# Seven products of half matrices for eight in the down projection of a fused retention and gated feed-forward kernel

## The chip, the cores and the metric

The kernel runs on one core of a Trainium2 chip. The metric is device time in microseconds. TensorE (PE) multiplies matrices into PSUM, VectorE (DVE) and ScalarE (ACT) read PSUM and write SBUF, GpSimd (POOL) and SyncE (SP) here mostly issue transfers. Each engine takes its instructions strictly in the order in which the kernel wrote them (PE may load weights a little ahead), and waits at semaphores for the others.

## The reference

```
gamma = 1.0 - 2.0 ** (-5.0 - arange(H))                     # B, H, S, D = 4, 8, 768, 64
for t in range(S):
    state = gamma * state + outer(k[:, :, t], v[:, :, t])
    y[:, :, t] = scale * q[:, :, t] @ state
x = y.transpose(0, 2, 1, 3).reshape(3072, 512)
gate = 1.0 / (1.0 + exp(-(x @ w_gate)))                     # w_gate, w_val: 512 x 1536
out = (gate * (x @ w_val)) @ w_out                          # w_out: 1536 x 512
```

Inputs and output are float32; the kernel multiplies in bfloat16 and sums in float32.

## The kernel before

Retention is computed in 24 chunks of 128 tokens (four batches of six), the feed-forward part in six tiles of 512 tokens, four chunks to a tile. A tile has 12 up groups, `up(t, n1)`: eight products of 512 columns into two PSUM banks (gate and value), a sigmoid on ACT into `gs`, and a product on DVE into `hT[t][:, n1]`, the transposed hidden rows in bfloat16. Then come eight down groups: for each of four blocks of 128 tokens two halves of six products of 512 columns into one bank (L316), a copy on ACT into `ob` (L321) and a store on SP. The last block of the last tile is computed by `last_down` in pieces of 256, 128 and 128 columns (L336), copied by DVE, ACT and DVE.

The attention work for later tiles is put between these groups by the table `plan`: an entry `(i, block, done, new)` runs after group `i`. `block(done, new)` finishes two chunks (`inter` L190 and `intra` L237 on PE, then `y_out` L245 on DVE, which writes a quarter of the next tile's `xT` each) and begins two others (`scores` L178 and `state` L196 on PE, `masks` L183 and L184 and `state_sum` L222 to L226 on DVE). On DVE the order in a block with both is the two `y_out`, four masks, the state sums. `casts` (L202) has ACT write the summed state into `zbd`, which later `inter` products read. `step_t` transposes a chunk on PE, copies it on ACT into `qkT` (L151), and scales `v` on DVE into `vs` (L169); from chunk 12 on SP's transfers do the transposes (`xbar`) and POOL the scaling. Chunk loads are issued by POOL.

Seven PSUM banks serve everything but the states, in rotation: the eighth request waits until the readers of the first are through. `gs` has three buffers, `hT` two, `ob` three. The order of instructions is written out by hand; no scheduler changes it. In tile 0 the first four up groups run ahead of the loop, so that its groups 0 to 7 are up and 8 to 15 down; in tile 1 the first ten up groups are done in two halves of 256 columns, the second half by `up_columns` (L299), 25 groups in all.

Of the kernel before, what the change touches and what calls it, by code (L numbers as in the profile page):

```python
# [17 lines left out]
def kernel(  # L18
# [22 lines left out]
    ctx.enter_context(tc.manual_schedule())  # L41
    const = ctx.enter_context(tc.tile_pool(name="const", bufs=1))
    wpool = ctx.enter_context(tc.tile_pool(name="wpool", bufs=1))
    ld = ctx.enter_context(tc.tile_pool(name="ld", bufs=12))
    at = ctx.enter_context(tc.tile_pool(name="at", bufs=2))
    ffn = ctx.enter_context(tc.tile_pool(name="ffn", bufs=3))
    pz = ctx.enter_context(tc.tile_pool(name="pz", bufs=1, space=bass.MemoryType.PSUM))
# [4 lines left out]
    NT = N_TOK // 512  # L52
# [23 lines left out]
    wo = wpool.tile([128, NFF, D_MODEL], BF16, name="wo")  # L76
# [9 lines left out]
                            in_=moe_w_out.rearrange("(n p) d -> p n d", p=128)[:, s * 3:(s + 1) * 3, :])  # L86


    kf = const.tile([C, H, D], F32, name="kf")
    qf = const.tile([C, H, D], F32, name="qf")  # L90
    nc.sync.dma_start(out=kf, in_=src(k, 0))
    nc.sync.dma_start(out=qf, in_=src(q, 0))
    nc.scalar.preload_act_table(AX.Exp)
# [42 lines left out]
    xT, vs, qkT, sc, stA, stB, y, zbds = {}, {}, {}, {}, {}, {}, {}, {}  # L136
    zz, za = {}, {}

    def bank(shape, dt=F32):
        return pf.tile(shape, dt, tag="ff", name="ff", padded_shape=[128, 2 * NP, C] if dt == BF16 else None)  # L140
# [18 lines left out]
            nc.scalar.activation(qkT[g][:, i * NP:(i + 1) * NP], tp, AX.Copy)  # L159

    def xbar(g):
        qkT[g] = ld.tile([128, 2 * NP, C], BF16, tag="qkX", name="qkX", bufs=8)
        for i, x in enumerate((kn[g], qn[g])):
            nc.sync.dma_start_transpose(out=qkT[g][:, i * NP:(i + 1) * NP, :],
                                        in_=x.rearrange("s h d -> s (h d)"))

    def scale_v(g, eng):
        vs[g] = ld.tile([C, H, D], BF16, tag="vs", name="vs", bufs=8)
        eng.tensor_tensor(vs[g], vf[g], tabv[:, g % NCH, :].unsqueeze(2).to_broadcast([C, H, D]),  # L169
                          op=ALU.mult)  # L170

# [104 lines left out]
    hT = {}  # L276
# [15 lines left out]
    def up_columns(t, n1s, lo, hi):  # L292
        n = hi - lo
        ps = []
        for w in (wg, wv):
            u = bank([128, 512])
            for i, n1 in enumerate(n1s):
                for kk in range(KT):
# [6 lines left out]
        nc.vector.tensor_tensor(hT[t][:, n1s[0]:n1s[-1] + 1, lo:hi], g.rearrange("p (i n) -> p i n", n=n),  # L305
                                ps[1].rearrange("p (i n) -> p i n", n=n), op=ALU.mult)

    po = {}

    def down(t, sm, part):  # L310
        if part == 0:
            po[0] = bank([128, 512])
        o = po[0]
        half = NFF // 2
        for n1 in range(part * half, (part + 1) * half):
            nc.tensor.matmul(o, hT[t][:, n1, sm * 128:(sm + 1) * 128], wo[:, n1, :],  # L316
                             start=(n1 == 0), stop=(n1 == NFF - 1))
        if part == 0:
            return
        ob = ffn.tile([128, D_MODEL], F32, tag="ob", name="ob")  # L320
        nc.scalar.copy(ob, o)  # L321
        row = t * 512 + sm * 128
        nc.sync.dma_start(out=out[row:row + 128, :], in_=ob)

    def keep_on(n):
        u = bank([128, 512])
        for _ in range(n):
            nc.tensor.matmul(u[:, :128], ident, ident, start=True, stop=True)  # L328

    def last_down(t):  # L330
        row = t * 512 + 384
        first = 0
        for i, width in enumerate((256, 128, 128)):
            o = bank([128, 512])
            for n1 in range(NFF):
                nc.tensor.matmul(o[:, :width], hT[t][:, n1, 384:512], wo[:, n1, first:first + width],  # L336
                                 start=(n1 == 0), stop=(n1 == NFF - 1))
            ob = ffn.tile([128, width], F32, tag=f"ob{width}", name="ob", bufs=2)
            if i == 1:
                nc.scalar.copy(ob, o[:, :width])  # L340
                nc.scalar.dma_start(out=out[row:row + 128, first:first + width], in_=ob)
            else:
                nc.vector.tensor_copy(ob, o[:, :width])
                nc.sync.dma_start(out=out[row:row + 128, first:first + width], in_=ob)
            first += width


    scale_v(0, nc.gpsimd)
# [64 lines left out]
    def ups(t):  # L413
        return [lambda n1=n1: up(t, n1) for n1 in range(NFF)]

    def downs(t):
        return [lambda sm=sm, i=i: down(t, sm, i) for sm in range(4) for i in range(2)]

    plan = {
        0: [(9, step_t, 4), (11, step_t, 5), (12, block, None, 4), (12, casts, 4), (13, step_t, 6), (14, block, 4, None)],  # L420
        1: [(0, step_t, 7), (2, block, None, 6), (3, step_t, 8), (4, casts, 6), (5, step_t, 9), (7, block, 6, 8),
            (9, casts, 8), (11, step_t, 10), (13, step_t, 11), (15, block, 8, 10), (17, casts, 10), (20, block, 10, None)],
        2: [(1, block, None, 12), (3, casts, 12), (7, block, 12, 14), (9, casts, 14), (16, block, 14, 16), (18, casts, 16)],
        3: [(6, block, 16, 18), (8, casts, 18), (15, block, 18, 20), (17, casts, 20)],
        4: [(6, block, 20, 22), (8, casts, 22), (14, block, 22, None)],
        5: [],
    }
    for t in range(NT):
        groups = ups(t) + downs(t)
        if t == NT - 1:  # L430
            groups[-2:] = [lambda: last_down(t)]
        if t == 0:
            groups = groups[4:]
            for g in range(8, 12):
                load_chunk(g)
        if t == 1:
            groups[:10] = [lambda n1=n1: up(1, n1, 0, 256) for n1 in range(10)]
            groups[10:10] = [lambda n1=n1: up_columns(1, range(n1, n1 + 2), 256, 512) for n1 in range(0, 10, 2)]
            for g in range(12, 16):
                load_chunk(g)  # L440
        if t == 2:
            scale_v(14, nc.gpsimd)
            scale_v(15, nc.gpsimd)
            load_chunk(18)
            scale_v(16, nc.gpsimd)
            scale_v(17, nc.gpsimd)
            load_chunk(19)
        if t == 3:
            for g in range(18, 22):
                scale_v(g, nc.gpsimd)  # L450
            load_chunk(22)
# [50 lines left out]
```

## Time and profile before

| | |
|---|---|
| time, three runs | 234.22 us median, 233.8 to 235.6 |
| span of the profiled execution | 232.9 us (its own time on the device is the span and about a microsecond around it; the median is 1.3 above) |
| PE busy | 222.9 us, 96% of the span |
| DVE, ACT, POOL busy | 110.0, 91.8, 92.2 us |
| up products (L285), 512 columns | 452 recorded, 379 ns each with overlap |
| down products (L316), 512 columns | 267 recorded, 379 ns each with overlap |
| TensorE clock granted | full throughout |

In the views, a line such as `L316 PE MATMUL ff<-wo,hT` names the kernel's line, the engine, the operation, and what is written from what; `ff` is any of the seven banks. A matmul's length includes its way through the array, which overlaps the next one, so the distance between starts is its price. "Idle before" names what ended the engine's idle time. In the chain of waits, each row has a start, a length and the work; in the timeline, rows of one kind that follow each other are merged.

### The profile page before, as it was taken

Reading aid. Unit: us, or ns where it says so; the run is one execution under the profiler, and the core shown is the slowest. Engines: PE = TensorE matmul, PEld = TensorE weight load, DVE = VectorE, ACT = ScalarE, POOL = GpSimd, SP = SyncE. Lnnn points to the kernel's source line nnn. Section 1 sums busy time; section 2 is a strip of 40 time slices with the busy share of each in tenths; the row PEclk is TensorE's granted clock in tenths of the full one; section 3 lists DMA queues with packets and bytes.
Section 4 is the critical chain, followed back from the end, with each engine's and each line's share of the span. In section 5 each row is a group of like instructions: output and inputs, shape, how many; then the busy total and the mean of one; then the engine's idle time right before and its main releaser. Section 6 shows DMA issues by size and latency. Waiting matters only on the chain.

```text
span 232.9 us, 4448 instructions
## 1 busy us (share of the span) xinstructions
PE 222.9 (96%) x1781; PEld 125.5 (54%) x1802; DVE 110.0 (47%) x201; ACT 91.8 (39%) x177; POOL 92.2 (40%) x111
## 2 busy tenths in 40 slices
PE   6878999999999999999999999999999999999994
PEld 5654644557889645445445445445445454444444
DVE  4465533275996562284924445716236711244301
ACT  8765233354727332253522432522532422433221
POOL 8999864788899743495118200000000000000000
PEclk9999999999999999999999999999999999999999
DMA  7999999999999999999959953001200011100022
GB/s 135 187 188 173 197 202 204 183 234 231 215 175 155 114 114 125 276 180 143 107 70 160 205 101 61 1 30 63 91 0 3 0 45 69 69 0 0 0 93 90
DMA packets 77557, 27.29 MB, mean 117 GB/s; under 512 B 65057, under 2 KB 73121, under 8 KB 77537
## 3 DMA queue, kind: packets, MB, share of 16 engines
q0 software_dynamic: 57616, 16.78, 75.9%
q1 hardware_dynamic: 19776, 10.16, 22.2%
q8 instruction: 14, 0.23, 0.4%
q10 hardware_dynamic: 144, 0.07, 0.1%
q14 instruction: 7, 0.05, 0.1%
HBM read 28.31 MB, written 6.29 MB: 149 GB/s over the span
## 4 chain that ended last, share of the span: by engine, by line
PE 84%; POOL 6%; DMA 3%; issue 2%; DVE 2%; ACT 1%; POOLq 0%
PE ff L285 46%; PE ff L316 25%; PE ff L299 5%; DMA wv<-in_moe_w_val_dram 3%; PE ff L237 2%; PE ff L178 2%; PE ff L190 2%; PE ff L149 1%; PE ff L336 1%; POOL qn L68 1%; POOL kn L67 1%; PE z L196 1%; POOL vf L62 1%; POOL vs L169 1%; POOL wg L81 1%
## 5 line engine op out<-in xcount | busy, mean ns | idle before, releaser
L290 DVE TENSOR_TENSOR hT<-gs,ff 128x512 bf16<-128x512 f32 (+2 forms) x72 | 45.6, 641 | 69.4 <-PE ff L285 57.1
L285 PE MATMUL ff<-xT,wg 128*128 128x512 bf16 (+2 forms) x277 | 68.0, 361 | 1.4 <-DVE xT L245 0.7
L285 PE MATMUL ff<-xT,wv 128*128 128x512 bf16 (+2 forms) x287 | 68.6, 361 | 0.7 <-DMA wv<-in_moe_w_val_dram 0.6
L289 ACT ACTIVATE gs<-ff 128x512 f32<-128x512 f32 (+2 forms) x72 | 40.2, 562 | 68.0 <-PE ff L285 62.0
L316 PE MATMUL ff<-wo,hT 128*128 128x512 bf16 x267 | 61.1, 379 | 0.9 <-issue 0.5
L285 PEld LDWEIGHTS <-wv 128*128 128x128 bf16 x288 | 28.1, 98 | 29.8 <-DMA wv<-in_moe_w_val_dram 0.9
L316 PEld LDWEIGHTS <-hT 128*128 128x128 bf16 x276 | 26.3, 98 | 31.3 <-DVE hT L290 0.6
L285 PEld LDWEIGHTS <-wg 128*128 128x128 bf16 x288 | 27.1, 98 | 28.5 <-issue 0.7
L321 ACT COPY ob<-ff 128x512 f32<-128x512 f32 x23 | 13.5, 585 | 51.1 <-PE ff L316 38.2
L245 DVE TENSOR_TENSOR xT<-ff,taby 128x512 bf16<-128x512 f32 x24 | 15.6, 686 | 25.9 <-PE ff L237 25.9
L169 POOL TENSOR_TENSOR vs<-vf,tabv 128x512 bf16<-128x512 f32 x14 | 14.7, 1060 | 26.0 <-DMA vf<-in_v_dram 22.9
L62 POOL DMA_DIRECT2D vf<-in_v_dram x23 | 20.8, 904 | 8.1 <-DMA kn<-in_k_dram 2.8
L67 POOL DMA_DIRECT2D kn<-in_k_dram x23 | 21.0, 912 | 3.2 <-DMA wo<-in_moe_w_out_dram 1.1
L68 POOL DMA_DIRECT2D qn<-in_q_dram x23 | 20.5, 892 | 3.1 <-DMA wo<-in_moe_w_out_dram 2.2
L183 DVE TENSOR_TENSOR stA<-ff,causal 128x512 bf16<-128x512 f32 x24 | 16.3, 681 | 2.7 <-PE ff L178 2.6
L184 DVE TENSOR_TENSOR stB<-ff,causal 128x512 bf16<-128x512 f32 x24 | 16.3, 679 | 0.0
L202 ACT CAST zbd<-za 64x256 bf16<-64x256 f32 x32 | 12.9, 403 | 8.6 <-DVE za L224 8.0
L169 DVE TENSOR_TENSOR vs<-vf,tabv 128x512 bf16<-128x512 f32 x10 | 7.3, 734 | 5.0 <-DMA vf<-in_v_dram 4.9
L151 ACT ACTIVATE qkT<-ff 128x1024 bf16<-128x1024 bf16 x8 | 8.2, 1026 | 1.6 <-PE ff L149 1.6
L328 PE MATMUL ff<-ident 128*128 128x128 bf16 x82 | 7.3, 254 | 1.6 <-POOL ident masks.py:199 1.6
L237 PE MATMUL ff<-stB,vs 128*64 128x128 bf16 x96 | 7.9, 222 | 0.4 <-DVE stB L184 0.4
L237 PE MATMUL ff<-stA,vs 128*64 128x128 bf16 x96 | 8.1, 222 | 0.0
(62 smaller groups left out, 141.5 us busy)
## 6 DMA issues: line engine op xcount, KB each, us to landing
vf<-in_v_dram POOLq DMA_DIRECT2D x23, 256.0 KB, 8.0
out_dram<-ob SPq DMA_DIRECT2D x23, 256.0 KB, 3.1
kn<-in_k_dram POOLq DMA_DIRECT2D x23, 128.0 KB, 7.8
qn<-in_q_dram POOLq DMA_DIRECT2D x23, 128.0 KB, 8.0
wg<-in_moe_w_gate_dram POOLq DMA_DIRECT2D x6, 256.0 KB, 7.5
wv<-in_moe_w_val_dram POOLq DMA_DIRECT2D x6, 256.0 KB, 8.0
wo<-in_moe_w_out_dram POOLq DMA_DIRECT2D x4, 384.0 KB, 11.4
kf<-in_k_dram SPq DMA_DIRECT2D x1, 256.0 KB, 3.4
```

What stands on the lines that cost most here:

```text
L62: eng.dma_start(out=vf[g], in_=src(v, g))
L67: nc.gpsimd.dma_start(out=kn[g], in_=src(k, g))
L68: nc.gpsimd.dma_start(out=qn[g], in_=src(q, g))
L169: eng.tensor_tensor(vs[g], vf[g], tabv[:, g % NCH, :].unsqueeze(2).to_broadcast([C, H, D]), op=ALU.mult)
L183: nc.vector.tensor_tensor(stA[g], sc[g][0], causal4, op=ALU.mult)
L184: nc.vector.tensor_tensor(stB[g], sc[g][1], causal4, op=ALU.mult)
L237: nc.tensor.matmul(y[g][i * D:(i + 1) * D, p, :], vs[g][:, 2 * p + i, :], st[:, p, :], start=(first and p == 0), stop=True, skip_group_che ...
L245: nc.vector.tensor_tensor(xT[g // 4][:, :, col:col + C], y[g], taby[:, :, c * C:(c + 1) * C], op=ALU.mult)
L285: nc.tensor.matmul(u[:, lo:hi], w[:, kk, n1 * 128:(n1 + 1) * 128], xT[t][:, kk, lo:hi], start=(kk == 0), stop=(kk == KT - 1))
L289: nc.scalar.activation(gs[:, lo:hi], ps[0][:, lo:hi], AX.Sigmoid)
L290: nc.vector.tensor_tensor(hT[t][:, n1, lo:hi], gs[:, lo:hi], ps[1][:, lo:hi], op=ALU.mult)
L316: nc.tensor.matmul(o, hT[t][:, n1, sm * 128:(sm + 1) * 128], wo[:, n1, :], start=(n1 == 0), stop=(n1 == NFF - 1))
```

## The change

From tile 1 on the down projection is done on half matrices. The 512 token columns of `hT` are split in halves of 256, the 12 row blocks into even and odd ones, and the 512 output columns into halves. With a11, a21 the even blocks of the first and second token half, a12, a22 the odd ones, b11, b12 the even blocks of `w_out` for the first and second half of the columns, and b21, b22 the odd ones, seven products of 6 x 256 columns are made for each of two token sub-blocks i, and the four quarters of the output are sums of them. `weight_sums` prepares four combinations of `w_out` in tile 0 (three calls, each for four blocks, with four operations on DVE and two copies on ACT). `hidden_sums` prepares three combinations of the hidden rows in `hs` and overwrites a21 by a11 - a21 (three calls a tile, four DVE operations each). `product` adds several products into the same bank, and `fast_out` takes intermediate values out of it: after product 2 a copy `p` of the bank on ACT and a sum on DVE, after 6 a copy and a sum and the first store, after 7 a sum, after 4 a copy and the second store.

There are now seven down groups in tiles 1 to 5, two products each. `last_down` is gone. In `plan`, the blocks of tiles 1 to 4 stand after other groups. `ld` has 11 buffers for 12, `qkX` and `vs` have 7 for 8, `ob` has 4 for 3, two of them used first by `kf` and `qf`.

```diff
-    ld = ctx.enter_context(tc.tile_pool(name="ld", bufs=12))
+    ld = ctx.enter_context(tc.tile_pool(name="ld", bufs=11))
...
-    kf = const.tile([C, H, D], F32, name="kf")
-    qf = const.tile([C, H, D], F32, name="qf")
+    kf = ffn.tile([C, H, D], F32, tag="ob", name="kf", bufs=4)
+    qf = ffn.tile([C, H, D], F32, tag="ob", name="qf", bufs=4)
...
-        qkT[g] = ld.tile([128, 2 * NP, C], BF16, tag="qkX", name="qkX", bufs=8)
+        qkT[g] = ld.tile([128, 2 * NP, C], BF16, tag="qkX", name="qkX", bufs=7)
...
-        vs[g] = ld.tile([C, H, D], BF16, tag="vs", name="vs", bufs=8)
+        vs[g] = ld.tile([C, H, D], BF16, tag="vs", name="vs", bufs=7)
...
+    wt = wpool.tile([128, 4, NFF // 2, 256], BF16, name="wt")
+    wo2 = wo.rearrange("p (f two) d -> p f two d", two=2)
+
+    def weight_sums(g):
+        fs = slice(2 * g, 2 * g + 2)
+        b11, b12 = (wo2[:, fs, 0, c:c + 256] for c in (0, 256))
+        b21, b22 = (wo2[:, fs, 1, c:c + 256] for c in (0, 256))
+        t3 = ffn.tile([128, 512], F32, tag="gs", name="gs").rearrange("p (f d) -> p f d", f=2)
+        t2 = ffn.tile([128, 512], F32, tag="gs", name="gs").rearrange("p (f d) -> p f d", f=2)
+        nc.vector.tensor_tensor(wt[:, 0, fs], b12, b11, op=ALU.subtract)
+        nc.vector.tensor_tensor(t3, b22, b12, op=ALU.subtract)
+        nc.scalar.copy(wt[:, 2, fs], t3)
+        nc.vector.tensor_tensor(t2, t3, b11, op=ALU.add)
+        nc.scalar.copy(wt[:, 1, fs], t2)
+        nc.vector.tensor_tensor(wt[:, 3, fs], b21, t2, op=ALU.subtract)
+
+    hs = {}
+
+    def hidden_sums(t, g):
+        if g == 0:
+            hs[t] = ffn.tile([128, 3, NFF // 2, 256], BF16, tag="hs", name="hs", bufs=1)
+        fs = slice(2 * g, 2 * g + 2)
+        h2 = hT[t].rearrange("p (f two) n -> p f two n", two=2)
+        a11, a21 = (h2[:, fs, 0, c:c + 256] for c in (0, 256))
+        a12, a22 = (h2[:, fs, 1, c:c + 256] for c in (0, 256))
+        s1, s2, s4 = (hs[t][:, i, fs] for i in range(3))
+        nc.vector.tensor_tensor(s1, a21, a22, op=ALU.add)
+        nc.vector.tensor_tensor(s2, s1, a11, op=ALU.subtract)
+        nc.vector.tensor_tensor(a21, a11, a21, op=ALU.subtract)
+        nc.vector.tensor_tensor(s4, a12, s2, op=ALU.subtract)
+
+    fast = {}
+
+    def product(t, i, n):
+        rows = [slice(c + i * 128, c + i * 128 + 128) for c in (0, 256)]
+        if n == 1:
+            fast[i] = (bank([128, 512]), bank([128, 512]))
+        a, c = fast[i][0][:, :256], fast[i][0][:, 256:]
+        to = {1: a, 2: fast[i][1][:, :256], 3: c, 4: a, 5: c, 6: a, 7: a}[n]
+        for f in range(NFF // 2):
+            h = lambda j, r: hT[t][:, 2 * f + j, rows[r]]
+            s = lambda j: hs[t][:, j, f, rows[0]]
+            w = lambda j, col: wo[:, 2 * f + j, col * 256:(col + 1) * 256]
+            left, right = {
+                1: lambda: (h(0, 0), w(0, 0)),
+                2: lambda: (h(1, 0), w(1, 0)),
+                3: lambda: (s(2), w(1, 1)),
+                4: lambda: (h(1, 1), wt[:, 3, f]),
+                5: lambda: (s(0), wt[:, 0, f]),
+                6: lambda: (s(1), wt[:, 1, f]),
+                7: lambda: (h(0, 1), wt[:, 2, f]),
+            }[n]()
+            nc.tensor.matmul(to, left, right, start=(f == 0 and n in (1, 2)), stop=(f == NFF // 2 - 1),
+                             skip_group_check=True)
+
+    def fast_out(t, i, n):
+        a, b = fast[i]
+        row = [t * 512 + c + i * 128 for c in (0, 256)]
+        if n == 2:
+            fast[i, "o"] = tuple(ffn.tile([128, D_MODEL], F32, tag="ob", name="ob", bufs=4) for _ in range(2))
+            fast[i, "p"] = ffn.tile([128, 512], F32, tag="p15", name="p15", bufs=2)
+            nc.scalar.copy(fast[i, "p"], a)
+            nc.vector.tensor_tensor(fast[i, "o"][0][:, :256], fast[i, "p"][:, :256], b[:, :256], op=ALU.add)
+        lo, hi = fast[i, "o"]
+        p1, p5 = fast[i, "p"][:, :256], fast[i, "p"][:, 256:]
+        if n == 6:
+            nc.scalar.copy(p1, a[:, 256:])
+            nc.vector.tensor_tensor(lo[:, 256:], p1, a[:, :256], op=ALU.add)
+            nc.sync.dma_start(out=out[row[0]:row[0] + 128, :], in_=lo)
+        if n == 7:
+            nc.vector.tensor_tensor(hi[:, 256:], p5, a[:, :256], op=ALU.add)
+        if n == 4:
+            nc.scalar.copy(hi[:, :256], a[:, :256])
+            nc.sync.dma_start(out=out[row[1]:row[1] + 128, :], in_=hi)
+
+    def products(t, *steps):
+        for i, n in steps:
+            product(t, i, n)
+            if n in (2, 6, 7, 4):
+                fast_out(t, i, n)
+
...
-        ob = ffn.tile([128, D_MODEL], F32, tag="ob", name="ob")
+        ob = ffn.tile([128, D_MODEL], F32, tag="ob", name="ob", bufs=4)
...
-    def last_down(t):
-        row = t * 512 + 384
-        first = 0
-        for i, width in enumerate((256, 128, 128)):
-            o = bank([128, 512])
...
-            if i == 1:
-                nc.scalar.copy(ob, o[:, :width])
-                nc.scalar.dma_start(out=out[row:row + 128, first:first + width], in_=ob)
-            else:
-                nc.vector.tensor_copy(ob, o[:, :width])
-                nc.sync.dma_start(out=out[row:row + 128, first:first + width], in_=ob)
...
     def downs(t):
+        if t > 0:
+            steps = [((0, 1), (0, 5)), ((0, 2), (1, 1)), ((1, 5), (1, 2)), ((0, 3), (0, 6)), ((1, 3), (1, 6)),
+                     ((0, 7), (1, 7)), ((0, 4), (1, 4))]
+            return [lambda st=st: products(t, *st) for st in steps]
         return [lambda sm=sm, i=i: down(t, sm, i) for sm in range(4) for i in range(2)]
...
         1: [(0, step_t, 7), (2, block, None, 6), (3, step_t, 8), (4, casts, 6), (5, step_t, 9), (7, block, 6, 8),
-            (9, casts, 8), (11, step_t, 10), (13, step_t, 11), (15, block, 8, 10), (17, casts, 10), (20, block, 10, None)],
-        2: [(1, block, None, 12), (3, casts, 12), (7, block, 12, 14), (9, casts, 14), (16, block, 14, 16), (18, casts, 16)],
-        3: [(6, block, 16, 18), (8, casts, 18), (15, block, 18, 20), (17, casts, 20)],
-        4: [(6, block, 20, 22), (8, casts, 22), (14, block, 22, None)],
+            (9, casts, 8), (11, step_t, 10), (13, step_t, 11), (16, block, 8, 10), (17, casts, 10), (23, block, 10, None)],
+        2: [(1, block, None, 12), (3, casts, 12), (7, block, 12, 14), (9, casts, 14), (18, block, 14, 16), (18, casts, 16)],
+        3: [(4, block, 16, 18), (8, casts, 18), (18, block, 18, 20), (18, casts, 20)],
+        4: [(4, block, 20, 22), (8, casts, 22), (11, block, 22, None)],
         5: [],
...
-        if t == NT - 1:
-            groups[-2:] = [lambda: last_down(t)]
...
-            if i == len(groups) - 9:
+            if i == (9 if t == 0 else len(groups) - 8):
...
             group()
+            if t == 0 and i in (9, 11, 13):
+                weight_sums((i - 9) // 2)
+            if t == 1 and i in (11, 13, 16):
+                hidden_sums(t, (11, 13, 16).index(i))
+            if t > 1 and i in (3, 7, 11):
+                hidden_sums(t, i // 4)
             for at_group, step, *g in plan[t]:
                 if at_group == i:
                     step(*g)
```

More of the change, by code (lines that the diff above doesn't have):

```diff
@@ L328, in keep_on @@
             nc.tensor.matmul(u[:, :128], ident, ident, start=True, stop=True)
-    def last_down(t):
-        row = t * 512 + 384
-        first = 0
-        for i, width in enumerate((256, 128, 128)):
-            o = bank([128, 512])
[L335 to L338, printed above, removed]
-            if i == 1:
-                nc.scalar.copy(ob, o[:, :width])
-                nc.scalar.dma_start(out=out[row:row + 128, first:first + width], in_=ob)
-            else:
-                nc.vector.tensor_copy(ob, o[:, :width])
-                nc.sync.dma_start(out=out[row:row + 128, first:first + width], in_=ob)
-            first += width
     scale_v(0, nc.gpsimd)
```

## The prediction

> **What bounds the kernel now.** I read the page first for the busiest engine, then the chain in order of time for its pace, then the groups kept apart by shape for prices, then the timeline around the places the change touches. The page shows TensorE busy for 96% of the span at a full clock, the other engines under half; bound by PE, then, with little slack to give back.
>
> ```profile
> PE 222.9 (96%) x1781; PEld 125.5 (54%) x1802; DVE 110.0 (47%) x201; ACT 91.8 (39%) x177; POOL 92.2 (40%) x111
> PEclk9999999999999999999999999999999999999999
> ```
>
> The chain gives PE's true pace (busy time of one matmul overlaps the next): twelve 512-column products in 2.59 us, 0.216 each; thirty-two 256-column products, each with its own weight load, in 3.49 us, 0.109 each. Half the columns really cost half. It shows one hold of PE by DVE in tile 1, too: hT was late at 85.08.
>
> ```profile
> 43.53 2.59 PE ff L316 x12
> ...
> 71.66 3.49 PE ff L299 x32
> ...
> 84.47 0.61 DVE hT L290
> 85.08 0.05 issue
> 85.12 2.98 PE ff L316 x13
> ```
>
> Prices of DVE and ACT work, by shape (busy us, mean ns):
>
> ```profile
> L290 DVE TENSOR_TENSOR hT<-gs,ff 128x512 bf16<-128x512 f32 x58 | 39.4, 686 | 63.2 <-PE ff L285 53.3 <-ACT gs L289 9.9
> L290 DVE TENSOR_TENSOR hT<-gs,ff 128x256 bf16<-128x256 f32 x10 | 4.0, 416 | 2.4 <-ACT gs L289 2.4
> L122 DVE MEMSET zbd<- 128x256 uint32 x4 | 1.1, 272 | 0.1
> L321 ACT COPY ob<-ff 128x512 f32<-128x512 f32 x23 | 13.5, 585 | 51.1 <-PE ff L316 38.2 <-remote 5.7 <-DMA out_dram<-ob 4.3
> L289 ACT ACTIVATE gs<-ff 128x256 f32<-128x256 f32 x10 | 3.7, 386 | 4.0 <-PE ff L285 3.9
> ```
>
> Latencies and the places themselves come from the timeline (start, length, engine). At the tile end of the last tile PE passes from L285 to L316 at 219.27 and DVE starts the last hT at 219.54, 0.27 later, for 0.69. Independent 512-element DVE operations follow each other every 0.60 (masks at 81.67 and 82.27). Near 54 us the first product of tile 1 starts 0.06 after the last xT; DVE had only 0.59 us of idle time before that.
>
> ```profile
> 51.44 0.68 DVE L169 TENSOR_TENSOR vs<-vf,tabv 128x512 bf16<-128x512 f32 x1
> 52.71 1.29 DVE L245 TENSOR_TENSOR xT<-ff,taby 128x512 bf16<-128x512 f32 x2 [0.59 <-PE ff L237]
> 54.06 0.61 PE L285 MATMUL ff<-xT,wg 128*128 128x256 bf16 x4
> 81.67 0.68 DVE L183 TENSOR_TENSOR stA<-ff,causal 128x512 bf16<-128x512 f32 x1
> 82.27 0.68 DVE L184 TENSOR_TENSOR stB<-ff,causal 128x512 bf16<-128x512 f32 x1
> 219.27 2.11 PE L316 MATMUL ff<-wo,hT 128*128 128x512 bf16 x9
> 219.54 0.69 DVE L290 TENSOR_TENSOR hT<-gs,ff 128x512 bf16<-128x512 f32 x1 [1.04 <-PE ff L285]
> ```
>
> **Removed.** Tiles 1 to 4: 48 x 0.216 = 10.37 us of down products each become 84 x 0.109 = 9.16, saving 1.21 each. Tile 5: 7.77 + 2.66 (chain: L316 x36, L336 x36) become 9.16, saving 1.27. Together **-6.1 us**. The hold at 85.08 (PE due at 84.8) goes with the moved block: **-0.3**.
>
> **The unknown price.** Each hidden_sums is four DVE operations on 512 all-bf16 elements in SBUF; no row has one. Bounds: 0.27 (the memset, which writes 512 bf16 values as 256 words) and 0.69 (any 512-element row, so no pairing). I take 0.42, the 256-wide row, because the memset is counted in words of two values. A dependent one follows after 0.45, an independent one after 0.33. From the feed end of a tile's last up product (T = 0): hT 11 ends at 0.96, s1 at 1.41, s2 1.86, the difference 2.19, s4 2.52; DVE is free for the next operation at 2.43. weight_sums has two f32 intermediates, so I count 0.33 + 0.60 + 0.72 + 0.72 = 2.4 us.
>
> **Tile 0.** Three weight_sums enter DVE's queue and six copies (one each 0.49 behind the last) ACT's. The first two cost DVE nothing: it idled over 2 us before vs at 43.85 and 46.87. But qkT of chunk 5 on ACT stands behind two more copies: 47.63 to 48.66 instead of 46.64 to 47.67. scores of chunk 5, due at 48.14, start at 48.8; state_sum and masks shift by 0.77. The third weight_sums (2.4) then stands between the masks and the two xT operations; their 0.59 of slack is used first. 0.77 + 2.4 - 0.59: xT ends at 56.5 instead of 54.0, and PE has nothing else to do. **+2.5**.
>
> **Each fast tile.** Product 7 overwrites what product 6 left, so it waits for fast_out. For i = 0 two products cover it. For i = 1 only one (0.65): from the end of (1,6), 0.20 to ACT, copy 0.385, DVE 0.41, 0.06: 1.06. Hold 0.41; (1,4) waits 0.08 more for the DVE add behind (1,7). **5 x 0.49 = +2.5**. Product 5 needs s1 of the last group after ten of its tile's products, at 1.09; s1 plus 0.05 and an exposed weight load of 0.1 comes at about 1.53. Hold 0.43 in tiles 2, 3 and 5 (in 1 and 4 a block lies between): **+1.3**.
>
> **Moved blocks.** In tiles 1, 2 and 3 the block that completes the next tile's xT now stands after the last group, with no down work behind it. The next up product waits for both xT operations. After tile 1: inter 0.45, half of intra 0.28, latency 0.17, then xT at 0.90 and 1.50, ending at 2.19; PE is through at 1.02: 1.23. After tiles 2 and 3 scores stand between, so xT ends at 2.74 and PE is through at about 1.75 and 1.81: 1.05 and 1.0. **+3.3**. Before, four or three groups of down work lay behind them.
>
> Tile 1's block 8,10 stands behind hidden_sums: xT from 2.43, four masks from 3.63, za ends at 6.45; ACT's two zbd casts (0.41 each) wait for za, and fast_out's p copy stands behind the casts: 7.25 to 7.83. Product 3 writes over what p copies; it was due at 1.82 + 6 x 0.654 + 0.04 = 5.78 and starts at 7.88. **+2.1**. In tile 2, block 12,14 stands behind hidden_sums at group 7: its first xT ends at 3.12 and frees the bank that the second half of up 8 needs at 2.45: **+0.7**. In tiles 3 and 4 the block after group 4 finds its bank just free in time: nothing, with 0.7 each if the sums cost 0.69. Sums after groups 3 and 7 otherwise hide: DVE needs 0.69 of the 1.73 us of an up pair, and PE is three pairs ahead in banks.
>
> **Tail and queues.** The last product's copy (0.2 + 0.385) and its 256 KB (2.0 to landing in the quiet end, against 1.6 for 64 KB) replace a 128-column copy and store: **+0.5**; it would be 1.6 at the 3.1 median of all 256 KB stores. SP's xbar issues stand before the same groups as before; a fourth ob buffer spares ACT the 4.3 us it waited for a store, where PE didn't wait: nothing. vs has one buffer less: on POOL's queue chunk 21 now waits for chunk 14, and loads 22 and 23 behind it issue about 10 us later, still a tile before use: nothing; without that slack, one 8 us load.
>
> **A rule against it.** At 72.89 DVE's vs operation took 1.12 us beside a POOL vs run (71.40 to 73.46); alone it takes 0.68, so 0.44 a meeting. Every sum reads SBUF twice, and ten POOL vs run between 71 and 134. I count nothing, since the early groups' sums have 1 us of slack; three exposed meetings would be 1.3. The Trainium skill (SBUF — State Buffer, Who interferes with whom) says that a DVE instruction with two SBUF inputs and a GpSimd one that reads SBUF exclude each other for the whole instruction. By it a meeting could cost as much as the POOL operation's remaining length, up to 1.04 here, and three would be 3.1 as an estimate.
>
> **Sum.** -6.1 - 0.3 + 2.5 + 2.5 + 1.3 + 3.3 + 2.1 + 0.7 + 0.5 = +6.5 us on the span of 232.9, so 239.4. The median of the runs lies 1.3 above the profiled span; I keep that: **240.7 us**. With sums at 0.27: s1 0.15 less three times, 0.5 less in tiles 1 and 2 each, 0.1 in tile 0: 239.2. With 0.69: s1 0.27 more three times, 1.08 in tiles 1 and 2 each, 0.7 in tiles 3 and 4 each, 0.3 in tile 0: 245.4.
>
> **Rivals.** (A) The sums run unpaired: 245.4. For it: every 512-element row, whatever its sources, lies near 0.69. Against: the memset. 15%. (B) Not slower: holds of one tile overlap, because while PE is held DVE and ACT empty their queues. If only the longest of each tile counts (2.5, 2.1 - 0.3, 1.05, 1.0, 0.49, 0.49) the sum is 7.3 + 0.5 - 6.1 = +1.7: 235.9, inside what can't be told from no change. It decides from 4 us of overlap on. Against: the waits hang on different operations, each timed from PE's own arrival. 17%. (C) Faster: DVE and ACT stay ahead everywhere except at the round trip of product 7: -6.1 - 0.3 + 2.5 + 0.5 = -3.4: 230.8. For it: both engines are under half busy. Against: an average; the queues are strictly in order at the four places above. 7%. (D) The products don't reach half price: each 0.01 us over 0.109 costs 4.2; the L299 row speaks against. 5%.
>
> My forecast has 56%. A measurement of this kernel tells about 1% (2.3 us) from no change. Half of B lies within 1%, the rest over it, so slower 0.84, same 0.09, faster 0.07. The range: 236.0 takes in most of B, 244.8 most of A.
>
> **What would show it.** Right: PE idle about 2 us before the first L285 of tile 1, about 2 us before product 3 of tile 1, about 1 us before the first L285 of tiles 2, 3 and 4; hidden_sums near 0.42; products 0.109 apart. Wrong: these pauses under half of that, sums near 0.27 or 0.69, or a pause at a place not named.

## The result, and the profile after

The changed kernel takes **243.72 us** in the median of four runs (241.97 to 245.45), against 234.01 (233.76 to 235.6) for the kernel before beside it: a ratio of **1.040, 95% interval 1.035 to 1.046**. Slower, as forecast; 3.0 us above the predicted 240.7, inside the range. The profiled execution took 243.32 with a span of 241.6. Throughout, executions more than 1.5% above the fastest of their kernel count as slow and the ratios leave them out (two of the four in experiment 3, two of the seventeen of the kernel before beside experiments 9 and 10), while medians and ranges are of all.

The page's first rows, of the kernel after:

```profile
PE 220.5 (91%) x1958; PEld 141.5 (59%) x1958; DVE 152.6 (63%) x301; ACT 96.5 (40%) x193; POOL 92.7 (38%) x111
...
PEclk9999999999999999999999999999999999999998
```

TensorE is busy for 2.4 us less than before, in a span 8.7 us longer. Its idle share went from 4% to 9%; DVE's busy time went from 110.0 to 152.6. A hold, in what follows, is a time in which PE has nothing to do but wait. The view of PE's waits (engine, tile and line; what it waited for; us in total, times, longest) says where PE stood:

```profile
PE ff L285 <- DVE xT L245: 7.6, 6, 2.1
PE ff L360 <- ACT p L369: 2.0, 1, 2.0
...
PE ff L360 <- DVE ob L375: 1.3, 5, 0.3
...
PE ff L360 <- DVE xT L245: 0.8, 1, 0.8
PE ff L360 <- DVE hs L334: 0.7, 3, 0.2
...
PE ff L285 <- DVE hT L290: 0.3, 1, 0.3
```

All of these rows are new, except that L285 waited for xT once before, for 0.7 in total. Where PE waits for xT it can be for the data, or for the PSUM bank that the xT operation reads. The timeline gives each its place (start, length, engine and line; in brackets PE's idle time just before and its releaser):

```profile
56.16 0.61 PE L285 MATMUL ff<-xT,wg 128*128 128x256 bf16 x4 [1.62 <-DVE xT L245]
...
86.64 1.47 PE L360 MATMUL ff<-wo,hT 128*128 128x256 bf16 x12 [0.78 <-DVE xT L245]
...
91.42 0.82 PE L360 MATMUL ff<-wo,hs 128*128 128x256 bf16 x6 [2.00 <-ACT p L369]
92.07 0.82 PE L360 MATMUL ff<-wt,hs 128*128 128x256 bf16 x6
92.73 0.82 PE L360 MATMUL ff<-wo,hs 128*128 128x256 bf16 x6
...
95.11 2.14 PE L360 MATMUL ff<-wt,hT 128*128 128x256 bf16 x18 [0.26 <-DVE ob L375]
...
99.43 0.81 PE L285 MATMUL ff<-xT,wg 128*128 128x512 bf16 x3 [1.16 <-DVE xT L245]
...
119.14 1.02 PE L285 MATMUL ff<-xT,wv 128*128 128x512 bf16 x4 [2.14 <-DVE xT L245]
...
138.07 1.04 PE L285 MATMUL ff<-xT,wg 128*128 128x512 bf16 x4 [1.04 <-DVE xT L245]
...
149.03 1.02 PE L285 MATMUL ff<-xT,wg 128*128 128x512 bf16 x4 [0.34 <-DVE hT L290]
...
173.79 1.04 PE L285 MATMUL ff<-xT,wg 128*128 128x512 bf16 x4 [0.92 <-DVE xT L245]
```

Products of six matmuls start 0.65 apart (91.42, 92.07, 92.73): 0.109 for each matmul, half price. The last of the six ends 0.82 after the first start, so a bracket counts about 0.16 less than the delay by starts: product 7 was due at 92.73 + 18 x 0.109 = 94.69 and began at 95.11, 0.42 late with 0.26 in the bracket. This is also why PE's busy time fell by less than the products save. The pauses of 1.62, 2.00, 1.16, 1.04 and 0.92 lie where the prediction put them. Those it had wrong are 0.78 at the head of tile 1's products, 2.14 in tile 2 and 0.34 in tile 3.

The starts of the tiles sum it up (first L285 of each tile; lengths are their differences, worked out here):

| | tile 0 | tile 1 | tile 2 | tile 3 | tile 4 | tile 5 and end |
|---|---|---|---|---|---|---|
| before | 54.06 | 40.18 | 35.61 | 34.70 | 34.00 | 34.35 |
| after | 56.16 | 43.27 | 38.64 | 35.72 | 33.25 | 34.56 |
| difference | +2.1 | +3.1 | +3.0 | +1.0 | -0.75 | +0.2 |
| forecast | +2.5 | +2.3 | +1.5 | +0.7 | -0.7 | +0.15 |

Tiles 4 and 5, where no block stands at the end of the tile, gain or nearly break even; the loss lies in the first four, and what exceeds the forecast lies in tiles 1, 2 and 3.

### The profile page after: what moved, and what is told of

It is laid out like the page before. It is cut to its first block, busy times and chain, and to the rows that moved or that the text cites. A ratio compares the mean times of both kernels' runs of the same rounds, so it can differ in the third digit from the quotient of the medians.

```text
span 241.6 us, 4908 instructions
## 1 busy us (share of the span) xinstructions
PE 220.5 (91%) x1958; PEld 141.5 (59%) x1958; DVE 152.6 (63%) x301; ACT 96.5 (40%) x193; POOL 92.7 (38%) x111
## 4 chain that ended last, share of the span: by engine, by line
PE 50%; DVE 10%; ACT 2%; issue 1%; DVEq 0%
PE ff L285 32%; PE ff L360 15%; DVE xT L245 3%; DVE hT L290 2%; DVE stA L183 1%; DVE stB L184 1%; PE ff L190 1%; PE ff L237 1%; PE ff L178 1%; DVE ob L375 1%; ACT zbd L202 1%; ACT p L374 1%; DVE hs L334 1%; DVE hs L337 1%; DVE hs L335 1%
## 5 line engine op out<-in xcount | busy, mean ns | idle before, releaser
L285 PE MATMUL ff<-xT,wg 128*128 128x512 bf16 (+2 forms) x288 | 68.9, 362 | 5.8 <-DVE xT L245 5.5
L285 PE MATMUL ff<-xT,wv 128*128 128x512 bf16 (+2 forms) x288 | 68.8, 361 | 2.1 <-DVE xT L245 2.1
L285 PEld LDWEIGHTS <-wv 128*128 128x128 bf16 x288 | 28.1, 98 | 31.4 <-issue 2.4
L285 PEld LDWEIGHTS <-wg 128*128 128x128 bf16 x288 | 27.0, 98 | 33.1 <-DVE xT L245 4.3
L169 POOL TENSOR_TENSOR vs<-vf,tabv 128x512 bf16<-128x512 f32 x14 | 15.2, 1092 | 45.5 <-PE ff L237 36.0
L360 PEld LDWEIGHTS <-hT 128*128 128x128 bf16 x240 | 23.2, 98 | 6.6 <-issue 3.1
L62 POOL DMA_DIRECT2D vf<-in_v_dram x23 | 20.8, 904 | 6.4 <-DVE hs L337 1.6
L360 PEld LDWEIGHTS <-hs 128*128 128x128 bf16 x180 | 17.4, 98 | 5.6 <-issue 2.2
L360 PE MATMUL ff<-wt,hs 128*128 128x256 bf16 x120 | 16.9, 273 | 0.7 <-DVE hs L334 0.7
L360 PE MATMUL ff<-wo,hT 128*128 128x256 bf16 x120 | 15.6, 273 | 0.8 <-DVE xT L245 0.8
L360 PE MATMUL ff<-wt,hT 128*128 128x256 bf16 x120 | 14.8, 272 | 1.3 <-DVE ob L375 1.3
L369 ACT COPY p<-ff 128x512 f32<-128x512 f32 x10 | 5.8, 586 | 14.1 <-PE ff L360 14.0
L397 PE MATMUL ff<-wo,hT 128*128 128x512 bf16 x48 | 11.4, 379 | 0.0
L375 DVE TENSOR_TENSOR ob<-p,ff 128x256 f32<-128x256 f32 x10 | 4.2, 421 | 10.4 <-ACT p L374 10.4
```

The source lines that it names most:

```text
L62: eng.dma_start(out=vf[g], in_=src(v, g))
L285: nc.tensor.matmul(u[:, lo:hi], w[:, kk, n1 * 128:(n1 + 1) * 128], xT[t][:, kk, lo:hi], start=(kk == 0), stop=(kk == KT - 1))
L360: nc.tensor.matmul(to, left, right, start=(f == 0 and n in (1, 2)), stop=(f == NFF // 2 - 1), skip_group_check=True)
```

## The price of a sum, and what stands beside it

The groups of the sums, by line and shape (busy us, mean ns):

```profile
L336 DVE TENSOR_TENSOR hT<-hT 128x512 bf16<-128x512 bf16 x15 | 8.0, 531 | 0.0
L335 DVE TENSOR_TENSOR hs<-hs,hT 128x512 bf16<-128x512 bf16 x15 | 7.2, 480 | 0.5
...
L334 DVE TENSOR_TENSOR hs<-hT 128x512 bf16<-128x512 bf16 x15 | 6.4, 424 | 0.5
```

A sum takes 0.42, the value taken. The means of the others come from single instructions three times as long. In tile 2, DVE's timeline and POOL's of the same kernel:

```profile
115.26 0.42 DVE L334 TENSOR_TENSOR hs<-hT 128x512 bf16<-128x512 bf16 x1
115.72 1.25 DVE L335 TENSOR_TENSOR hs<-hs,hT 128x512 bf16<-128x512 bf16 x1
116.89 1.26 DVE L336 TENSOR_TENSOR hT<-hT 128x512 bf16<-128x512 bf16 x1
118.07 0.41 DVE L337 TENSOR_TENSOR hs<-hT,hs 128x512 bf16<-128x512 bf16 x1
118.41 1.28 DVE L245 TENSOR_TENSOR xT<-ff,taby 128x512 bf16<-128x512 f32 x2
```

```profile
115.65 2.22 POOL L169 TENSOR_TENSOR vs<-vf,tabv 128x512 bf16<-128x512 f32 x2 [7.47 <-PE ff L237]
```

L335 begins 0.07 after the first of two POOL vs, and L336 beside the second: L336 ends only 0.28 after POOL is through. A sum beside a POOL vs is called a meeting below. The releaser in POOL's row says what brought these together: with seven vs buffers, POOL waits for a product (L237) of an earlier use of vs, and that comes from the block whose group these sums stand in. Tile 1 has one such meeting (L336 took 1.26 at 84.39) and tile 3 one (L337, 1.26 at 147.12).

The profiles of the experiments, taken together, show that the three holds follow the meetings. Tile 3's hold is there in the four profiles with a long sum ahead of it (0.34 here, 0.25, 0.34 and 0.37 in experiments 1, 5 and 8) and in none of the others. In tile 1 the bank is waited for in every profile with the products in this order and a meeting (0.78 to 1.34), and not in experiment 1, which has none. Tile 2's hold is 2.14 wherever two sums are long and 1.29 in the two profiles (1 and 6) where one is.

## Experiments

Theory: the halved products save what was forecast, and the holds do not overlap; each comes off by itself when its own cause is moved. The rivals: the holds share one cause (a full DVE queue), so removing one lengthens another; or the time went elsewhere. A hold is taken from a profile, of one execution, the time from all runs. The first four were timed against 234.15 (233.87 to 234.9) for the kernel before, the next four against 234.06 (233.61 to 234.78), the last two against 233.94 (233.63 to 239.04).

**1. Tile 1's zbd casts three groups later.**

```
-(17, casts, 10)
+(20, casts, 10)
```

> One entry of the plan moved: the casts of chunk 10 stand after group 20 instead of 17, so that on ACT both p copies of tile 1 stand ahead of them. Theory (ACT's strict order makes PE wait): the 2.00 us hold before product 3 of tile 1 (profile of the changed kernel, PE waiting for ACT's p copy) is gone, and the span falls by 2.0 us. Rival (holds of one tile overlap): the wait only moves, to the add behind the masks on DVE or to the bank of the next product, and the span falls by under 1 us.

Measured: 241.43 (239.63 to 242.36), ratio 1.030 [1.024, 1.034]. The 2.00 hold of L360 by p is gone from the profile. In the changed kernel's profile ACT had it so, the casts waiting for the summed state and the copies p behind them:

```profile
89.94 0.82 ACT L202 CAST zbd<-za 64x256 bf16<-64x256 f32 x2 [7.41 <-DVE za L224]
90.78 1.07 ACT L369 COPY p<-ff 128x512 f32<-128x512 f32 x2
```

The median fell by 2.3. The span of the profiled execution, the fastest of the four, fell by 3.7, more than one hold: in this execution tile 1's sums met no POOL operation (its hold of 0.78 is missing) and only one of tile 2's did, 1.29 in place of 2.14. Together 2.00 + 0.78 + 0.85 = 3.6. The casts stand behind tile 1's sums in the program, so the edit can't have taken that meeting away: meetings come and go from run to run.

**2. The weight sums one group earlier.**

```
-if t == 0 and i in (9, 11, 13):
+if t == 0 and i in (8, 10, 12):
```

> The three weight_sums stand after groups 8, 10 and 12 of tile 0 instead of 9, 11 and 13. Theory: the third one no longer stands between the masks and xT, so tile 1's first product starts at about 54.1 to 54.5 us instead of 56.16; span 1.7 to 2.0 us less. Rival (DVE's total load counts, not the place): the masks are late by as much as xT was, PE waits for them instead, and tile 1 starts at 55.5 or later.

Measured: 241.89 (240.68 to 242.54), ratio 1.032 [1.028, 1.036]. Tile 1 starts at 54.35 in place of 56.16, so the forecast hold was real. But tile 1 gave much of it back. DVE's timeline, POOL's, then PE's of this kernel:

```profile
81.93 2.54 DVE L334 TENSOR_TENSOR hs<-hT 128x512 bf16<-128x512 bf16 x1
```

```profile
82.12 2.06 POOL L169 TENSOR_TENSOR vs<-vf,tabv 128x512 bf16<-128x512 f32 x2
```

```profile
84.53 0.39 PE L360 MATMUL ff<-wt,hs 128*128 128x256 bf16 x2 [0.54 <-DVE hs L334]
...
86.26 2.29 PE L360 MATMUL ff<-wo,hT 128*128 128x256 bf16 x12 [1.34 <-DVE xT L245]
```

One sum stood through both POOL operations, 2.54 in place of 0.42, and product 5 and the bank behind it waited 0.54 and 1.34. After that the row of the granted clock by stretches shows 0.50 from 87 to 90. That cost little here: the copies p, late behind the same sum, came at 90.40 to 91.47, and PE, slower, waited for them for 0.33 in place of 2.00.

**3. The blocks at tile ends earlier or split.**

```
-(23, block, 10, None)
+(21, block, 10, None)
-(18, block, 14, 16)
+(16, block, 14, None), (18, block, None, 16)
-(18, block, 18, 20)
+(16, block, 18, None), (18, block, None, 20)
```

> The attention blocks that complete the next tile's xT are put ahead of the last down groups: in tile 1 block 10,None after group 21 instead of 23; in tiles 2 and 3 the finishing half of the block after group 16, the beginning half stays after 18. Theory: the three holds of the next tile's first product (1.16, 1.04, 0.92 us in the profile of the changed kernel) go; span 3.1 us less. Rival: xT's work on DVE now delays fast_out's sums, and the round trip of product 7 grows from 0.4 to 1 us or more in these tiles; span within 1.5 us.

Measured: 240.40 (237.33 to 241.56), ratio 1.018 [1.011, 1.025]. The three end-of-tile holds (1.16, 1.04, 0.92, together 3.1) are gone; the row of L285 waiting for xT is down to 4.5 in three waits. The ratio rests on two runs, 239.67 and 237.33, in the mean 5.2 under the changed kernel's median; the trace accounts for 3.1, and the rest is open. The profiled execution, at 241.56, lost part of the gain to the clock: after the pause of 2.14 in tile 2 the granted clock was 0.50 for over 3 us (experiment 7 shows the same). Columns: stretch, its length, busy time and instructions of PE, PEld, DVE, ACT and POOL, granted clock, DMA share, GB/s.

```profile
119.00:120.00 1.00, 1.00 (x4) 0.32 (x3) 1.00 (x3) 0.00 (x0) 0.00 (x0) 0.50 1.32 261
120.00:121.00 1.00, 1.00 (x4) 0.31 (x3) 1.00 (x3) 0.19 (x1) 0.00 (x0) 0.50 0.19 30
121.00:122.00 1.00, 1.00 (x4) 0.45 (x3) 0.97 (x3) 0.96 (x3) 0.00 (x0) 0.50 0.00 0
```

PE counts as busy throughout, with four matmuls in a stretch instead of the six or seven from 110 to 113. Only the clock row tells.

**4. The copy of product 3 made at once (a miss).**

```
-if n == 6: copy(p1, a[:, 256:])
+if n == 3: copy(p1, a[:, 256:])
```

> fast_out's second copy (the half bank that product 3 completes) is issued right after product 3 instead of after product 6. Theory (the round trip after product 6 is ACT copy plus DVE add): only the add is left of it, 0.27 + 0.42 + 0.05 against 0.65 of cover, so the hold before product 7 of i = 1 falls from 0.42 to about 0.1 in five tiles; span 1.6 us less. Rival (the hold is only the DVE add and its latency): no change beyond 0.3 us. The copy waits for the p copy's readers on DVE, so in tile 1, where those are late, no gain is expected.

Measured: 248.62 (248.27 to 249.21), ratio 1.061 [1.059, 1.064]: slower. I had thought that product 6, which writes the other half of the bank, was free to run beside the copy. The view of PE's waits says no:

```profile
PE ff L360 <- ACT p L374: 4.6, 10, 0.5
```

The wait is for the whole bank: in all ten halves product 6 stood behind the copy with nothing in between. Tiles 4 and 5 together took 1.9 us longer than in the changed kernel (69.67 against 67.81).

**5. Tile 2's sums behind the block.**

```
-if t > 1 and i in (3, 7, 11): hidden_sums(t, i // 4)   # ahead of the block
+if (t, i) == (2, 7): hidden_sums(t, 1)                 # behind the block
```

> In tile 2 the four sums of group 7 stand behind the block of chunks 12 and 14 on DVE's queue instead of ahead of it. Theory (the sums keep the block's first xT off DVE, and two of them take 1.25 us instead of 0.42 beside a POOL vs): the 2.14 us wait of L285 for xT in tile 2 goes, and with it the clock drop that can follow it; the time falls by about 2, to 241.7 in the median and 240 at a full clock. Rival (the bank is late for another reason, such as the block's own PE work): the wait stays over 1.4 and the time within 0.5 of the changed kernel.

Measured: 240.84 (240.40 to 241.04), ratio 1.028 [1.026, 1.031]. The wait of 2.14 is gone; tile 2 lasts 36.42 in place of 38.64. The four runs lie within 0.64 us, where the changed kernel's spread over 3.5; whether that is the pause's doing isn't shown, for experiments 4 and 8, which keep it, lie within 0.94 and 0.90.

**6. An eighth vs buffer.**

```
-tag="vs", name="vs", bufs=7
+tag="vs", name="vs", bufs=8     # and 10 loads in the ld pool in place of 11
```

> vs gets its eighth buffer back (the ld pool's loads give one up for the room). Theory (with seven buffers POOL's vs of chunks 19 and 20 wait for a product of the very block at which the sums run, so that they meet; with eight they run earlier): L335 and L336 of group 7 in tile 2 take 0.42 to 0.45 instead of 1.25, the wait of L285 there falls from 2.14 to about 0.7, as I had forecast without the meeting; the time falls by 1.4. Rival (the sums are slow by themselves there, or the meeting only moves to the neighbouring sums): the wait stays near 2, the time within 0.5.

Measured: 242.24 (241.91 to 244.44), ratio 1.037 [1.032, 1.042]; no gain that the times can tell. POOL's timeline and DVE's, then PE's:

```profile
116.12 1.04 POOL L169 TENSOR_TENSOR vs<-vf,tabv 128x512 bf16<-128x512 f32 x1 [8.12 <-PE ff L237]
119.38 1.04 POOL L169 TENSOR_TENSOR vs<-vf,tabv 128x512 bf16<-128x512 f32 x1 [2.22 <-DMA vf<-in_v_dram]
```

```profile
116.20 1.24 DVE L335 TENSOR_TENSOR hs<-hs,hT 128x512 bf16<-128x512 bf16 x1
117.37 0.41 DVE L336 TENSOR_TENSOR hT<-hT 128x512 bf16<-128x512 bf16 x1
```

```profile
118.77 1.02 PE L285 MATMUL ff<-xT,wv 128*128 128x512 bf16 x4 [1.29 <-DVE xT L245]
```

Half right. One of the two POOL operations still waits for the same product and still meets L335; the other doesn't run beside L336, which takes 0.41 again, and the hold falls by 0.85, which is how much longer that one sum had been. With both gone it would come to 1.29 - 0.83 = 0.46, an estimate, near the 0.7 forecast without meetings. How much of this is the buffer's doing stays open: POOL's eighth vs from chunk 12 on did run earlier (106.97, without that wait), but experiment 1 had the same hold of 1.29 with seven buffers, because there a later load (117.17) kept the second vs away.

**7. Product 5 one product later.**

```
-((0, 1), (0, 5)), ((0, 2), (1, 1)), ...
+((0, 1), (1, 1)), ((0, 5), (0, 2)), ...
```

> Product 5 of the first half comes one product later (behind product 1 of the second half). Theory (product 5 is held 0.39 us by s1 of the last group in tiles 2, 3 and 5, with 0.65 us of work that could go ahead): those three holds go, -1.2 us. Rival (s1 is late by more than one product, or holding costs nothing since another hold behind it takes its place): the time stays within 0.4, and an equal wait appears at product 2 or 5.

Measured: 243.0 (241.82 to 243.79), ratio 1.038 [1.033, 1.042], which by itself tells nothing. The row of PE waiting for hs (0.7, 3 times) is gone from the profile, and tiles 4 and 5 up to the last products take 0.39 less (174.41 to 236.01, against 173.79 to 235.78). In tile 1 the hold at the bank is longer (1.4 against 0.8) and the one at p shorter (1.3 against 2.0), since they follow each other: what the one gains the other loses. The gain of three holds was lost to the clock in this execution: after tile 2's 2.14 pause it was 0.54, 0.50, 0.50 and 0.75 in the four stretches from 120 to 124, 1.7 us of PE's time.

**8. The copy of product 3 covered by the other half's product.**

```
-((0, 3), (0, 6)), ((1, 3), (1, 6)),        copy at n == 6
+((0, 3), (1, 3)), ((0, 6), (1, 6)),        copy at n == 3
```

> The copy of what product 3 left is made right after product 3, and the products are put in the order 3, 3, 6, 6 of the two halves, so that the other half's product covers each copy. Theory (the round trip of product 7 costs 0.49 for each tile because copy, add and semaphores take 1.06 and only 0.65 covers them): from product 6 on only the add remains (0.20 + 0.41 + 0.06 = 0.67 against 0.65 of cover), so the hold of 0.42 falls under 0.1 and that of 0.08 stays: -1.6 to -2 us over five tiles. Rival (PE waits for the whole bank, so the copy is waited for by product 6 as when it was moved alone, and the order only spreads the waits): ten waits of about 0.4 or more remain and the time is not under the changed kernel's.

Measured: 241.84 (241.65 to 242.55), ratio 1.034 [1.030, 1.037]. The row of L360 waiting for ob is gone and no row for the copy replaces it. PE's timeline, end of tile 1:

```profile
92.97 1.47 PE L360 MATMUL ff<-wt,hs 128*128 128x256 bf16 x12
94.37 2.80 PE L360 MATMUL ff<-wt,hT 128*128 128x256 bf16 x24
```

Twelve matmuls of 0.109 from 92.97 end at 94.28, so 0.09 remains of the hold of 0.42: 0.33 a tile, 1.65 over five. In tile 1 the wait at the bank is 0.34 longer (1.12, two sums having met POOL), and the spans agree: 241.6 to 240.3. That it works here, and not alone, fits experiment 4: the copy made early needs another product over it.

**9. All of these together, without the eighth buffer.**

> All edits that took a hold away in a profile, together: casts behind the products, weight_sums one group earlier, the blocks at the ends of tiles 1 to 3 split or moved two groups earlier, tile 2's sums of group 7 behind the block, the covered copy and product 5 one product later. Theory (the time behind the halved products went into holds that do not overlap, so they come off one by one): from the changed kernel's profiled span of 241.6 go 2.0 (p copy), 1.8 (tile 0 to 1), 3.1 (tile ends), 2.1 (tile 2's bank), 1.6 (round trips), 1.2 (s1): 229.8, and a time of about 231.5, 1% under before; up to 1.1 more if tile 1's sums meet POOL's vs as they did when weight_sums alone was moved. Rival (the holds replace one another, since DVE's queue is the common cause): the single gains do not add, and the time stays over 236.

Measured: **232.21** (231.24 to 234.53, twelve runs), ratio **0.992 [0.989, 0.996]**: 4.7% under the changed kernel and level with the kernel before, 0.8% under it, which is less than the 1% that the prediction takes a measurement to tell. The page, and the longest of PE's waits for DVE:

```profile
PE 220.6 (96%) x1958; PEld 142.3 (62%) x1958; DVE 152.9 (66%) x301; ACT 97.4 (42%) x193; POOL 92.3 (40%) x111
...
PEclk9999999999999999999999999999999999999999
```

```profile
PE ff L360 <- DVE xT L245: 0.8, 1, 0.8
...
PE ff L285 <- DVE xT L245: 0.7, 1, 0.7
PE ff L360 <- DVE hT L290: 0.6, 1, 0.6
```

The same arithmetic on the same engines, PE idle for 4% as before the change; the 0.7 of L285 was there before, too. The span went from 241.6 to 231.0: 10.6 of the 11.8 expected. The gains add but for about a tenth, so most of the holds were separate, and the rival, over 236, falls. Of the missing 1.2, 0.64 is a new hold in tile 2: the sums put behind the block met a POOL vs there (L337, 1.27 at 116.28), and hT behind them came late for L360. Another 0.4 is tile 0's, which ends 1.4 earlier where 1.8 was expected. The 0.8 at tile 1's bank stays although no sum of tile 1 is long in this profile; there product 5, now later, no longer stands ahead of the wait, which made it 0.65 longer in experiment 7. Tile 4 now takes 32.92 (164.26 to 197.18) against 34.00 before the change: 1.08 of the 1.21 forecast for the products alone.

**10. The last third of the weight sums in tile 1 (a miss).**

```
-if t == 0 and i in (8, 10, 12): weight_sums((i - 8) // 2)
+if (t, i) in ((0, 9), (0, 11), (1, 9)): weight_sums(2 if t else (i - 9) // 2)
```

> The same, but weight_sums of the first two thirds stay at groups 9 and 11 of tile 0 and the last third goes to group 9 of tile 1. Theory (the 1.6 us pause ahead of tile 1 is DVE's queue, 2.4 of it the last weight_sums, and in tile 1 DVE has time for it): tile 1 starts at about 54.5 in place of 56.2 and the meeting of L334 with POOL's vs in tile 1 stays away or short: 229 to 231.5, not slower than the version above. Rival (tile 1's DVE queue is full as well, so the last third comes back as a hold there): the time lies 1 to 2.4 over the version above.

Measured: 238.10 (237.51 to 239.28), ratio 1.017 [1.013, 1.021]. Tile 1 starts at 54.51, as expected, but in experiment 9 it had started at 54.76 already, so 0.25 was all there was to win. Then one meeting spread over three engines. DVE's timeline, ACT's and PE's:

```profile
70.84 2.97 DVE L317 TENSOR_TENSOR wt<-wo 128x512 bf16<-128x512 bf16 x1
```

```profile
74.45 0.62 ACT L319 CAST wt<-gs 128x512 bf16<-128x512 f32 x1 [6.29 <-DVE gs L318]
...
75.70 1.64 ACT L202 CAST zbd<-za 64x256 bf16<-64x256 f32 x4
77.37 1.08 ACT L304 ACTIVATE gs<-ff 128x512 f32<-128x512 f32 x2
```

```profile
78.02 1.87 PE L299 MATMUL ff<-xT,wg 128*128 128x256 bf16 x8 [4.15 <-ACT gs L304]
```

The loss against experiment 9, 5.9, is over the rival's range too. L317, whose like takes 0.42, stood through two POOL vs (71.46 to 73.52 in POOL's timeline); ACT's copies waited for DVE in ACT's queue, four zbd casts behind them, the sigmoid behind those, and PE behind the sigmoid: 4.15. The granted clock was then 0.50 from 78 to 83 and 0.74 in the next stretch, 2.8 us more of PE's time. 4.15 + 2.8 is the 6.6 by which its span exceeds that of experiment 9, and a little over. (Its profiled execution was the slowest of the six.)

## Why the prediction was right, and where its sum was short

Pauses are idle time from the brackets; products 5 and 7 are delays by starts, product 5's from experiment 7.

| step | forecast | measured |
|---|---|---|
| one matmul of a product | 0.109 | 0.109 |
| a sum, alone | 0.42 (0.27 to 0.69) | 0.42 |
| tile 0 to 1 | +2.5 | +2.1 (tile 0's length; 1.8 of it off in experiment 2) |
| product 3 of tile 1 behind p | hold of 2.1 | 2.00 |
| tile ends 1, 2, 3 | 1.23, 1.05, 1.0 | 1.16, 1.04, 0.92 |
| product 5 behind s1 | 0.43, three times | 0.39, three times |
| product 7's round trip, i = 1 | 0.41 | 0.42 (0.33 of it off in experiment 8) |
| tile 1, bank at the first products | none | 0.78 |
| tile 2, second half of up 8 | 0.7 | 2.14 |
| tile 3, hT behind the sums | none | 0.34 |

The direction and the mechanism held: a saving of 6.1 in the products (tile 4, whose only hold is product 7's, shows 0.75 + 0.42 = 1.17 of its 1.21), paid for more than twice over in waits at places with nothing else for PE to do. The time by itself wouldn't have told this from rival A: 243.72 lies nearer to its 245.4 than to 240.7. The row of 424 ns and the places of the pauses do. One of the prediction's own signs of being wrong did come: pauses at places not named, 0.78 and 0.34.

**The term that failed is the meetings with POOL, counted at nothing.** The last three rows exceed their forecast by 0.78 + 1.44 + 0.34 = 2.6, and they lie in the tiles that came out too long, by 0.8, 1.5 and 0.3. Tile 0 took 0.4 less than forecast, and the span came out 2.2 above the 239.4 of the sum. The other 0.8 of the 3.0 lies between the profiled span and the median, 2.1 here against 1.3 before. The paragraph "I count nothing, since the early groups' sums have 1 us of slack" erred twice. The slack belongs to sums with no block behind them; behind group 7 of tile 2 stands one, and there I had myself found PE waiting. (The ten POOL vs of that paragraph are ten rows; two of them hold two operations each, so there are twelve.) And the 0.44 read from one row of before is no price of a meeting, but what happened to be left of a POOL operation: that DVE vs began at 72.89, POOL's ended at 73.46. The price is the rest of POOL's operation: 0.83 for one (1.25 - 0.42), 2.1 for a run of two (2.54 - 0.42, experiment 2). It can be more: sums that began 0.46 to 0.72 ahead of POOL's vs in the trace, while POOL was issuing a transfer (L62) just before it, were held to its end all the same, for 1.85, 2.08, 2.00 and 1.80 in experiments 3, 6, 8 and 10.

The Trainium skill (SBUF — State Buffer, Who interferes with whom) had said this: whichever of a DVE instruction with two SBUF inputs and a GpSimd one that reads SBUF comes first keeps the other out for its whole length. The runs agree that a sum is held to the end of the POOL operation, 1.25 beside one POOL vs and 2.54 and 2.97 beside two. That whichever comes first wins they don't show: the four sums above, and those of 2.54 and 2.97, began ahead of POOL's vs by the trace and were held; whether POOL's recorded starts are exact enough to tell is open. The estimate of 3.1 that I had set beside the nothing was nearer to the 2.6.

I had also dismissed the seventh vs buffer as "nothing", looking only at the loads. In the changed kernel two POOL vs were released by the block's product and met the sums; with the eighth buffer one of them ran earlier, though experiment 1 leaves open how much of the 1.44 this explains.

**The rivals.** (A) Unpaired sums: refuted by 424 ns. (B) Overlapping holds: refuted by experiment 9, where they add; inside tile 1 alone two of them share, since what lengthens the first shortens the second (experiment 7: 1.4 + 1.3 against 0.8 + 2.0). (C) Engines that stay ahead: refuted for the kernel as changed; experiment 9 reaches 231.0 in span by moving steps alone. (D) Dearer products: refuted at 0.109.

**Left open.** What share of tile 2's excess the seventh vs buffer has. What decides whether the clock falls after a pause (below), and so how the changed kernel's 241.97 to 245.45 divides between meetings and clock, since only one of its four runs has a trace.

## What to carry to other kernels

When PE is 96% busy, halving its work in a stage is worth only as much as there is other work for PE while the new results travel: price each new operand and each bank reuse from PE's arrival to its release, and give it another product to run behind. A sum of two SBUF operands on DVE cost its own 0.42 here only where no POOL vs ran beside it; ask of every buffer count you lower which POOL operations it will move, and beside what. Ask last what stands queued in order with a late copy: casts ahead of the copies made the 2.0, and casts and a sigmoid behind them the 4.15.

## What the runs showed of the hardware

In four profiles the granted clock fell to 0.50 for over 3 us after PE had paused for 1.9 to 2.5 us in all; others with the same pauses kept it full. (In a fifth, experiment 10, it fell during the pause of 4.15.) The same pause of 2.14 in tile 2 was followed by it in the profiles of experiments 3 and 7, and not in those of the changed kernel, 2, 4 and 8; a pause of 2.00 with 0.46 more soon after it was followed by it in experiment 4 (0.50 from 93 to 95), the same 2.00 without the 0.46 in the changed kernel was not, and 0.54 and 1.34 close together were in experiment 2. I had not counted on it, since in the profile before the clock was full throughout. In these four PE's work took about 1.7 us more each; in experiment 2 most of that came out of a wait that was due anyway. The Trainium skill (TensorE: Matmul & The Clock Gate, the table under Why this matters for your kernels) asks for no idle gaps over about 3 us; here pauses of 2.14 were enough in some executions.

PE's wait on a bank that ACT is reading is for the whole bank, as this kernel is built, even where it writes the half that isn't read: ten waits of 0.46 in experiment 4.
